# Half masks and two of five rank counts moved from VectorE to ScalarE in a top-k attention and mixture-of-depths kernel

## The chip, the cores and the metric

The kernel runs on one core of a Trainium2 chip. The metric is device microseconds of one execution. Engine names in the profile: PE is TensorE (PEld its weight loads), DVE is VectorE, ACT is ScalarE, POOL is GpSimd, SP is SyncE, which here only issues DMAs. Each engine works through its own queue in order.

## What is computed

There are B = 8 batches, 8 heads, S = 576 tokens and a head size of 64. Attention keeps the 32 largest scores of each row; the result, with the heads side by side, is the input `x` (576 x 512 per batch) of a mixture of depths: a gate picks 128 tokens of each batch, these go through a two-layer network, and the result is added to their rows.

```python
scores = scale * np.matmul(q, k.transpose(0, 1, 3, 2))
kth = np.partition(scores, -32, axis=-1)[..., -32:-31]
attn = softmax(np.where(scores >= kth, scores, -1e9))
x = np.matmul(attn, v)                      # (B, S, H*D)
gate = np.einsum('bsd,d->bs', x, w_gate)
for b in range(B):
    top_idx = np.argpartition(-gate[b], 128)[:128]
    xe = x[b, top_idx]
    ye = np.maximum(xe @ w1, 0.0) @ w2
    out[b, top_idx] = xe + sigmoid(gate[b, top_idx])[:, None] * ye
```

## The kernel before

**Units and steps.** The queries of a batch are cut into five tiles `t`: four of 128 tokens and a last one of 64 (`J` = 4 is the last). One unit is two heads of a tile (or four heads of the short tile), so a batch has 18 units (`per_batch`) and the whole kernel 144. The main loop (line 1143) makes one step per unit and works on units in different stages in each step `n`:

- PE multiplies the scores of unit n+1, and ACT copies them from PSUM to SBUF (`keep`, tile `sc`).
- DVE finds a bound for unit n by MAX8 over sevenths of each row and two rounds over the candidates (`find_bound`, line 527; tiles `cand`, `best`, `bound`).
- ACT takes, for unit n-1, the sign of every score against the bound and sums the signs (`part`, line 561; tiles `sides`, `seen`). POOL multiplies scores by these signs and appends eight steps (`weigh_signs`, tile `y`).
- DVE takes the eight largest of each row of `y` for unit n-2 (`find_kth`, tile `next`); the eighth is the 32nd largest score.
- For unit n-3 the mask of the scores below it is made (`mask`, line 585; tile `less`): the first head by ACT (Relu), the second by POOL. PE adds a large negative number at these places while it transposes the scores in step n+1.
- For unit n-4 ACT takes Exp (`pT`, `last`), PE multiplies by the values, ACT copies the sums out (`xs`).

**The mixture.** When all tiles of a batch have been divided by their sums and their gates computed, `mixture` (line 761) begins. It is a generator that is advanced at written-out steps of the following batches (`mix_at`, line 1023; `mix_at_of` for the last ones). First the gates go to DRAM and come back as a row on all partitions (`gate_row`). Then, for each tile, `choose` (line 800) counts on DVE how many gates of the row are larger than each gate of the tile: its rank. The scratch output is `junk`. A token with rank r goes into slot r, if r < 128: `pick[:, t, :]` is 1 where `slot` equals the rank, made by DVE for tile 0 (line 815) and by POOL for the others (`choose_slot`). PE multiplies `pick` by `parts` (the token's number and its gate, split into three bf16 pieces each), which gives for every slot the token and its gate; ACT copies that to `found`. Then POOL fetches the 128 rows by an indirect DMA, PE runs the two layers in small pieces, and POOL adds the rows to the output by another indirect DMA.

**What sets the order.** The order on each engine is the program's order, written out by hand. Lists hold work back: `vector_late` runs in the middle of the bound's search on DVE, `late` on ACT after the mask of step n (before the copies of loads and `sc`), `pool_late` on POOL after its half mask and before the products `y`. In the six `scatter_steps` (line 1041), in which POOL issues the indirect DMA that adds the rows, the second half mask goes to DVE through `vector_late` instead of POOL (lines 597 to 612 and 1207).

**The end.** The last batch has a path of its own (from line 1278), with counts split into `ranks` and `others`. At the very end DVE reduces a set of checks into `sure` (lines 1489 to 1511): among them, that all ranks and others add up to 8 x 576 x 575 / 2, which holds when no two gates are equal. If a check fails, a branch (line 1641) recomputes all batches in a general way.

Of the kernel before, what the change touches and what calls it, by code (L numbers as in the profile page):

```python
# [10 lines left out]
AF = mybir.ActivationFunctionType  # L11
ALU = mybir.AluOpType
FP32 = mybir.dt.float32
BF16 = mybir.dt.bfloat16
# [5 lines left out]
CAP = 128  # L20
# [28 lines left out]
def kernel(  # L49
# [11 lines left out]
    nc = tc.nc  # L61
    P = nc.NUM_PARTITIONS
    B, H, S, D = q.shape
# [3 lines left out]
    NT = J + 1  # L67
# [3 lines left out]
    DE = D + 1  # L71
    NDC = HD // P
    NFC = F // P
    scale = 1.0 / float(D) ** 0.5 / SMALLER
# [3 lines left out]
    const = ctx.enter_context(tc.tile_pool(name="const", bufs=1))  # L78
# [40 lines left out]
    for i in range(2):  # L119
        gate = const.tile([P, NT], FP32, name=f"gate{i}")  # L120
        nc.gpsimd.memset(gate, 0.0)
        parts = const.tile([P, NT, 2, 3], BF16, name=f"parts{i}")
        nc.gpsimd.memset(parts, 0.0)
        nc.vector.tensor_copy(out=parts[:, :, 0, 0:2], in_=parts_i)
        gates_of.append((gate, parts))
    slot_i = const.tile([P, CAP], I32, name="slot_i")
    nc.gpsimd.iota(slot_i, pattern=[[1, CAP]], base=0, channel_multiplier=0)
# [25 lines left out]

    ranks = const.tile([P, B, NT], FP32, name="ranks")
    nc.gpsimd.memset(ranks, 0.0)

    others = const.tile([P, NT], FP32, name="others")
    nc.gpsimd.memset(others, 0.0)
# [31 lines left out]
    def compare(out, in0, scalar, op, total=None):  # L190
        if total is None:
            total = stats.tile([P, 1], FP32, name="some")[0 : out.shape[0], :]
        dve.tensor_scalar(
            out=out,
            in0=in0,
            scalar1=scalar,
            scalar2=None,
            op0=op,
            op1=ALU.add,
            accum_out=total,  # L200
        )

    late, vector_late, pool_late = [], [], []
# [180 lines left out]
    def bank(pool, name, **how):  # L384
        return pool.tile([P, 512], FP32, name=name, **how)
# [199 lines left out]
    def mask(sc, next8, on=None):  # L585

        less = wkpool.tile([P, 2, S], BF16, name="less")  # L590
        for i, engine in enumerate(on or (act, pool)):
            kth = next8[:, i, 7:8]
            if engine is act:
                act.activation(less[:, i, :], sc[:, i, :], AF.Relu, bias=kth, scale=-1.0)
            else:

                def is_less(engine=engine, i=i, kth=kth):
                    if engine is None:
                        compare(less[:, i, :], sc[:, i, :], kth, ALU.is_lt)
                        return  # L600
                    engine.tensor_scalar(
                        out=less[:, i, :],
                        in0=sc[:, i, :],
                        scalar1=kth,
                        scalar2=None,
                        op0=ALU.is_lt,
                    )

                if engine:
                    is_less()  # L610
                else:
                    vector_late.insert(0, is_less)
        return less

    def turn_some(tr, z, less):
# [142 lines left out]
            rank[0:n, t : t + 1], rank[0:n, t : t + 1], tok[0:n, 1:2], ALU.add  # L758
        )

    def mixture(row0, pg, rank, exact=False):

# [28 lines left out]


        pick = modpool.tile([P, NT, CAP], BF16, name="pick")
        for t in range(NT):
            yield
            n = R if t == J else P

            def choose(t=t, n=n):  # L800
                junk = modpool.tile([P, S], FP32, name="junk", tag="scratch")
                dve.tensor_scalar(
                    out=junk[0:n, :],
                    in0=gate_row[0:n, :],
                    scalar1=gate[0:n, t : t + 1],
                    scalar2=None,
                    op0=ALU.is_gt,
                    op1=ALU.add,
                    accum_out=rank[0:n, t : t + 1],
                )  # L810
                if exact:
                    break_ties(t, gate, gate_row, rank)

                if t == 0:
                    compare(pick[:, t, :], slot, rank[:, t : t + 1], ALU.is_equal)
                else:
                    pool_late.append(lambda: choose_slot(t, n))

            def choose_slot(t, n):
                pool.tensor_scalar(  # L820
                    out=pick[0:n, t, :],
                    in0=slot[0:n, :],
                    scalar1=rank[0:n, t : t + 1],
                    scalar2=None,
                    op0=ALU.is_equal,
                )

            vector_late.append(choose)

# [2 lines left out]
            ps = ps_misc.tile([P, 512], FP32, name="place_ps", tag="misc")  # L832
        else:
            ps = values_bank[0]
        ps = ps[:, 2 * DE : 2 * DE + 6]


        done = B if exact else int(row0) // S + 1
        row_i = modpool.tile([P, 1], I32, name="row_i", bufs=2)
        g = modpool.tile([P, 1], FP32, name="g", bufs=2)  # L840
        multiply_places(ps, pick, pg)
        found = stats.tile([P, 6], FP32, name="found", bufs=2)
        place = stats.tile([P, 2], FP32, name="place", bufs=2)
        kept.append(lambda ps=ps: act.copy(out=found, in_=ps))

# [62 lines left out]
    def multiply_places(ps, pick, pg):  # L908

        for t in range(NT):  # L910
            n = R if t == J else P
            pe.matmul(
                ps,
                pick[0:n, t, :],
                pg[1][0:n, t, :, :].rearrange("p a e -> p (a e)"),
                start=(t == 0),
                stop=(t == J),
            )

    def split(gate, parts):  # L920

        rest = modpool.tile([P, NT], FP32, name="rest")
        pool.tensor_copy(out=parts[:, :, 1, 0], in_=gate)
        pool.tensor_tensor(rest, gate, parts[:, :, 1, 0], ALU.subtract)
        pool.tensor_copy(out=parts[:, :, 1, 1], in_=rest)
        pool.tensor_tensor(rest, rest, parts[:, :, 1, 1], ALU.subtract)
        pool.tensor_copy(out=parts[:, :, 1, 2], in_=rest)

    def add_parts(place, found):
        dve.tensor_reduce(  # L930
            out=place,
            in_=found.rearrange("p (a e) -> p a e", e=3),
            axis=mybir.AxisListType.X,
            op=ALU.add,
        )
# [12 lines left out]
    def fetch_rows(xe, of, row_i):  # L948
        pool.indirect_dma_start(
            out=xe,  # L950
            out_offset=None,
            in_=of.flatten_outer_dims(),
            in_offset=bass.IndirectOffsetOnAxis(ap=row_i, axis=0),
        )
# [182 lines left out]
    def mask_of(n, on=None):  # L1137
        b, i = divmod(n, per_batch)
        masks[n] = mask(scs[n], next8s[b][:, i, :, :], on)
        if i == per_batch - 1 and b < B - 1:  # L1140
            keep_least(b, bounds.pop(b)[:, :, :, 7], next8s.pop(b)[:, :, :, 7])

    for n in range(-1, N):
# [60 lines left out]
        if is_unit(n - 4):  # L1204
            turn_rest()()
        if is_unit(n - 3):
            mask_of(n - 3, (act, None) if n in scatter_steps else None)
        flush()
        if is_unit(n + 1) and n + 1 >= NHP:
            b, i = divmod(n, per_batch)  # L1210
# [55 lines left out]
        if gating is not None:  # L1266
            b, t = gating
            if t == J:
                store(out[b], of_batch[b][0])
                mixtures[b] = mixture(float(b * S), of_batch[b][1], ranks[:, b, :])  # L1270
        for b in rest:
            next(mixtures[b], None)
        b, i = divmod(n, per_batch)
# [153 lines left out]
    for t in (J - 1, J):  # L1427
# [6 lines left out]
            op0=ALU.subtract,  # L1434
            op1=ALU.is_equal,
        )
    ps = bank(ps_end, "av3")[:, 0:6]
    place = stats.tile([P, 2], FP32, name="place", bufs=2)
    row_i = modpool.tile([P, 1], I32, name="row_i", bufs=2)
    g = modpool.tile([P, 1], FP32, name="g", bufs=2)  # L1440
# [2 lines left out]
    keep_rows(place, row_i, float((B - 1) * S), float(B * S - 1))  # L1443
    xe = modpool.tile([P, HD], FP32, name="xe")
    fetch_rows(xe, out, row_i)
    dve.tensor_scalar_max(out=g, in0=place[:, 1:2], scalar1=-88.0)
    act.activation(g, g, AF.Exp, scale=-1.0)
    for _ in between:
# [42 lines left out]
    for what, op, than, limit in (  # L1491
        (bounded, ALU.min, ALU.is_gt, LEAST),
        (least, ALU.min, ALU.is_gt, LEAST),
        (low, ALU.min, ALU.is_gt, 0.5),
        (seen, ALU.max, ALU.is_lt, float(MIDDLE)),
        (seen, ALU.min, ALU.is_gt, float(MIDDLE - 16)),
        (sums.rearrange("p t h -> p (t h)"), ALU.min, ALU.is_gt, FEWEST),
        (sums.rearrange("p t h -> p (t h)"), ALU.max, ALU.is_lt, MOST),
    ):
        far = stats.tile([P, 1], FP32, name="far", bufs=2)  # L1500
        dve.tensor_reduce(out=far, in_=what, axis=mybir.AxisListType.X, op=op)
        dve.scalar_tensor_tensor(
            out=sure, in0=far, scalar=limit, in1=sure, op0=than, op1=ALU.mult
        )

    far = stats.tile([P, 1], FP32, name="far", bufs=2)
    dve.tensor_reduce(out=far, in_=ranks, axis=mybir.AxisListType.XY, op=ALU.add)
    dve.tensor_tensor(sure, sure, far, ALU.add)
    far = stats.tile([P, 1], FP32, name="far", bufs=2)
    dve.tensor_reduce(out=far, in_=others, axis=mybir.AxisListType.X, op=ALU.add)  # L1510
    dve.tensor_tensor(sure, sure, far, ALU.add)
    ones = stats.tile([P, 1], FP32, name="ones", bufs=1)
    dve.memset(ones, 1.0)
    unsure = const.tile([1, 1], I32, name="unsure")
# [2 lines left out]
    for f0 in range(0, NFC, 2):  # L1517
# [20 lines left out]
        out=unsure,  # L1538
        in0=ps[0:1, 0:1],
        scalar1=-1.0,  # L1540
        scalar2=float(P + B * (S * (S - 1) // 2)),
        op0=ALU.mult,
        op1=ALU.add,
    )
# [133 lines left out]
```

## Time and profile before

| | |
|---|---|
| median of 3 runs | 803.54 us (802.9 to 805.48) |
| the profiled execution | 802.83 us; span of its instructions 800.5 us; granted PE clock 0.997 |
| count on DVE (128 or 64 x 576) | 35 in the main loop, 788 ns; 83 ns more to read the accumulator |
| pick on DVE (128 x 128) | 7, 346 ns, and 83 ns |
| half mask on DVE (128 x 576) | 12 (6 in scatter steps, 6 at the end), 797 ns, and 82 ns |
| half mask on ACT | 141, 784 ns |
| half mask on POOL | 135, 1722 ns |
| sign with sum on ACT (`sides`) | 288, 797 ns, and 215 ns to read the accumulator |
| pick on POOL | 21 of 128 partitions, 609 ns |
| ACT_TABLE_LOAD | 1 |

A row of a group or of the timeline names line, engine, operation, what is written `<-` what is read. Most lines are L45, the helper that keeps program order, so groups are told apart by their tiles. In a timeline the first two numbers are the start and the time taken, both in microseconds; a bracket gives idle time of the engine before it and what ended that. Instructions of an engine overlap by a part of their durations, so the distance of two starts is what an instruction costs its queue. A row of waits reads: who, for whom, total in us, how many times, the longest.

### The profile page before, as it was taken

Reading aid. Unit: us, or ns where it says so; the run is one execution under the profiler, and the core shown is the slowest. Engines: PE = TensorE matmul, PEld = TensorE weight load, DVE = VectorE, ACT = ScalarE, POOL = GpSimd, SP = SyncE. Lnnn points to the kernel's source line nnn. Section 1 sums busy time; section 2 is a strip of 40 time slices with the busy share of each in tenths; the row PEclk is TensorE's granted clock in tenths of the full one; section 3 lists DMA queues with packets and bytes.
Section 4 is the critical chain, followed back from the end, with each engine's and each line's share of the span. In section 5 each row is a group of like instructions: output and inputs, shape, how many; then the busy total and the mean of one; then the engine's idle time right before and its main releaser. Section 6 shows DMA issues by size and latency. Waiting matters only on the chain. (4 is left out here: it accounts for less than half of the span.)

```text
span 800.5 us, 33285 instructions
## 1 busy us (share of the span) xinstructions
PE 728.1 (91%) x12535; PEld 550.2 (69%) x12535; DVE 771.6 (96%) x4655; ACT 728.4 (91%) x1577; POOL 706.4 (88%) x722
## 2 busy tenths in 40 slices
PE   8888888788999999999999989999899999999887
PEld 6766666656876668766786667866687667767756
DVE  7999999999999999999999999999999999999962
ACT  6999999999999999999999999999999999989830
POOL 4899999899999999999999999999999999999921
PEclk9999999999999999999999999999999999999999
DMA  8941114121241132221251221502234102101021
GB/s 170 293 95 43 42 62 103 29 54 29 70 107 42 29 94 63 64 55 41 69 109 29 56 41 62 113 20 54 42 90 89 29 8 75 24 6 25 3 74 31
DMA packets 121752, 50.70 MB, mean 63 GB/s; under 512 B 116016, under 2 KB 116016, under 8 KB 120560
## 3 DMA queue, kind: packets, MB, share of 16 engines
q1 hardware_dynamic: 118368, 43.94, 22.2%
q0 software_dynamic: 1744, 4.20, 2.8%
q8 instruction: 101, 1.65, 0.9%
q10 hardware_dynamic: 1472, 0.36, 0.2%
q14 instruction: 67, 0.55, 0.2%
HBM read 36.93 MB, written 11.55 MB: 61 GB/s over the span
## 5 line engine op out<-in xcount | busy, mean ns | idle before, releaser
L45 POOL TENSOR_TENSOR y<-sc,sides 128x576 f32<-128x576 f32 x288 | 366.9, 1304 | 17.7 <-ACT sides L45 16.6
L45 DVE MAX8 cand<-sc 128x8 f32<-128x82 f32 (+1 forms) x2016 | 314.4, 228 | 3.0 <-ACT sc L45 3.0
L45 POOL TENSOR_SCALAR less<-sc,next 128x576 bf16<-128x576 f32 x135 | 232.5, 1722 | 38.4 <-DVE next L45 34.2
L45 ACT ACTIVATE sides<-sc,bound 128x576 bf16<-128x576 f32 x288 | 229.6, 797 | 17.0 <-DVE bound L45 13.1
L45 PEld LDWEIGHTS av<-v,pT 128*64 128x64 f32 x4608 | 146.9, 138 | 91.4 <-ACT last L45 83.8
L45 DVE MAX8 next<-y 128x8 f32<-128x584 f32 x288 | 204.4, 751 | 0.0
L45 PE MATMUL av<-v,pT 128*64 128x65 f32 x4608 | 166.9, 225 | 38.9 <-ACT last L45 38.4
L45 PEld LDWEIGHTS <-less 64*128 64x128 bf16 (+1 forms) x2448 | 157.6, 129 | 29.3 <-POOL less L45 24.6
L45 PE MATMUL ps<-kT,qT 64*128 64x288 f32 (+1 forms) x1248 | 170.1, 422 | 0.3 <-ACT sc L45 0.3
L45 PE MATMUL ptr<-out_of_reach,less 64*128 64x64 bf16 x2272 | 151.0, 190 | 17.3 <-POOL less L45 16.6
L45 PE MATMUL ptr<-ident,sc 64*128 64x64 f32 x2272 | 166.3, 252 | 0.0
L45 ACT ACTIVATE pT<-ptr 128x1024 f32<-128x1024 f32 x142 | 147.7, 1040 | 14.5 <-PE ptr L45 12.7
L45 ACT COPY sc<-ps 128x1152 f32<-128x1152 f32 x140 | 159.6, 1140 | 0.0
L45 PEld LDWEIGHTS ptr<-ident,sc 64*128 64x128 f32 x2272 | 138.6, 137 | 23.8 <-issue 21.2
L45 ACT ACTIVATE less<-sc,next 128x576 bf16<-128x576 f32 x141 | 110.5, 784 | 0.0
L45 PEld LDWEIGHTS ps<-kT,qT 64*128 64x128 f32 (+1 forms) x1248 | 92.8, 176 | 17.6 <-ACT sc L45 0.4
L45 DVE MATCH_REPLACE8 cand<-best,cand 128x21 f32<-128x21 f32 (+1 forms) x576 | 98.8, 179 | 0.0
L45 DVE MAX8 best<-cand 128x8 f32<-128x21 f32 (+1 forms) x576 | 90.4, 189 | 0.0
L45 ACT ACTIVATION_READ_ACCUMULATOR sides<-sc,bound 128x1 f32 x288 | 62.0, 215 | 0.0
L45 PE MATMUL h_ps<-xeT,w 128*128 128x128 f32 x464 | 61.9, 278 | 0.0
L45 PEld LDWEIGHTS av<-ident,sc 128*128 128x128 f32 x144 | 20.0, 139 | 54.8 <-issue 44.9
L45 PE MATMUL av<-vpair,last 128*64 128x130 f32 x576 | 56.9, 276 | 0.0
(165 smaller groups left out, 925.2 us busy)
## 6 DMA issues: line engine op xcount, KB each, us to landing
v<-in_v_dram SPq DMA_DIRECT2D x64, 128.0 KB, 3.7
out_dram<-x SPq DMA_DIRECT2D x8, 1024.0 KB, 4.1
rows<-in_k_dram SPq DMA_DIRECT2D x56, 128.0 KB, 2.8
rows<-in_q_dram SPq DMA_DIRECT2D x56, 128.0 KB, 2.9
w<-in_moe_w_dram SPq DMA_DIRECT2D x2, 2048.0 KB, 10.3
gate_row<-row_dram SPq DMA_DIRECT2D x7, 288.0 KB, 4.6
last<-in_q_dram SPq DMA_DIRECT2D x8, 128.0 KB, 3.6
vpair<-in_v_dram SPq DMA_DIRECT2D x16, 64.0 KB, 4.8
```

The costliest lines, as they stand in the source:

```text
L45: return lambda *a, **kw: self._tc.keep_in_program_order(fn(*a, **kw))
```

## The change

**Half mask.** In the scatter steps both half masks are made by ACT (Relu, as the first half always was); DVE makes none in the main loop.

**Ranks of tiles 0 and 1.** In batches 0 to 6 DVE no longer counts for these two tiles. ACT takes the sign of (gate minus each gate of the row), with its sum: the sum is the number of smaller gates less the number of larger ones, 575 - 2 x rank. It is queued through `late`; its scratch output is the front of `pick`, which is filled later. The sums land in `signs`.

**Slots.** POOL compares `slot_signs` (575 - 2 x slot) with these sums, for both tiles after the sign of tile 1. So POOL makes the pick of tile 0, too. Tiles 2 to 4 stay as they were.

**Check.** `parts` has a seventh column of ones, so the matmul also tells how many tokens each slot got; ACT's copy goes to `places`, one row of seven numbers for each batch. At the end two reductions ask that each of these counts lies between 0.5 and 1.5; they stand in place of the two sums of ranks.

In the queues this means: per batch, DVE loses two counts and a pick (and in six steps a mask), ACT gets two signs (and in six steps a mask), POOL gets one pick. The order of everything else in the main loop stays.

```diff
@@ mask
-                def is_less(engine=engine, i=i, kth=kth):
-                    if engine is None:
-                        compare(less[:, i, :], sc[:, i, :], kth, ALU.is_lt)
-                        return
...
-                if engine:
-                    is_less()
-                else:
-                    vector_late.insert(0, is_less)
+                engine.tensor_scalar(
+                    out=less[:, i, :],
+                    in0=sc[:, i, :],
+                    scalar1=kth,
+                    scalar2=None,
+                    op0=ALU.is_lt,
+                )
@@ mixture
+            def weigh_gates(t=t):
+                total = sign_sum[:, t : t + 1]
+                act.activation(
+                    pick.rearrange("p t c -> p (t c)")[:, 0:S],
+                    gate_row,
+                    AF.Sign,
+                    bias=gate[:, t : t + 1],
+                    scale=-1.0,
+                    accum_out=total,
+                )
+                if t == 1:
+                    for u in range(2):
+                        pool_late.append(
+                            lambda u=u: choose_slot(
+                                u, P, slot_signs, sign_sum[:, u : u + 1]
+                            )
+                        )
+
+            if t < 2 and not exact:
+                late.append(weigh_gates)
+                continue
...
-                if t == 0:
-                    compare(pick[:, t, :], slot, rank[:, t : t + 1], ALU.is_equal)
-                else:
-                    pool_late.append(lambda: choose_slot(t, n))
+                pool_late.append(lambda: choose_slot(t, n))
...
-        found = stats.tile([P, 6], FP32, name="found", bufs=2)
+        found = places[:, 0 if exact else done - 1, :]
@@ main loop
-            mask_of(n - 3, (act, None) if n in scatter_steps else None)
+            mask_of(n - 3, (act, act) if n in scatter_steps else None)
@@ last batch
+    act.copy(out=places[:, B - 1, 6:7], in_=ps[:, 6:7])
@@ checks at the end
+        (places[:, :, 6], ALU.min, ALU.is_gt, 0.5),
+        (places[:, :, 6], ALU.max, ALU.is_lt, 1.5),
...
-    dve.tensor_reduce(out=far, in_=ranks, axis=mybir.AxisListType.XY, op=ALU.add)
-    dve.tensor_tensor(sure, sure, far, ALU.add)
...
-    dve.tensor_reduce(out=far, in_=others, axis=mybir.AxisListType.X, op=ALU.add)
-    dve.tensor_tensor(sure, sure, far, ALU.add)
```

At the start four instructions are new: DVE makes `slot_signs` from `slot`, POOL sets the ones of both `parts` tiles and the whole of `places`.

## Prediction

> **What bounds the kernel now.** First the page's busy times, to see which engine could be the bound.
>
> ```profile
> PE 728.1 (91%) x12535; PEld 550.2 (69%) x12535; DVE 771.6 (96%) x4655; ACT 728.4 (91%) x1577; POOL 706.4 (88%) x722
> ```
>
> Four engines lie within 8% of one another, so an average decides nothing. The loop works batch by batch (18 steps), so next I cut out one settled batch (steps 72 to 89, from the DVE timeline) and asked for busy time by stretch, then for ACT's waits in it.
>
> ```profile
> 377.17:471.75 94.58, 89.32 (x1555) 66.89 (x1553) 94.44 (x576) 90.92 (x198) 88.18 (x88) 1.00 0.26 61
> ```
>
> The columns are window, length, then busy PE, PEld, DVE, ACT, POOL. DVE is idle 0.14 us of 94.58: its instruction count sets the period. ACT has 3.66 us free. Its waits:
>
> ```profile
> ACT sides L45 <- DVE bound L45: 2.2, 5, 0.6
> ACT pT L45 <- PE ptr L45: 0.8, 2, 0.5
> ```
>
> ACT waits mostly for DVE; the same question for DVE in this batch lists no wait at all. Third, the DVE timeline of step 8 and the start of step 9, with the work the change touches:
>
> ```profile
> 417.83 1.10 DVE L45 MAX8 cand<-sc 128x8 f32<-128x82 f32 x7
> 418.95 0.76 DVE L45 TENSOR_SCALAR_CACHE_REDUCE junk<-gate_row,gate 128x576 f32<-128x576 f32 x1
> 419.75 0.35 DVE L45 TENSOR_SCALAR_CACHE_REDUCE pick<-slot,ranks 128x128 bf16<-128x128 f32 x1
> 420.02 1.11 DVE L45 MAX8 cand<-sc 128x8 f32<-128x82 f32 x7
> 423.76 1.39 DVE L45 MAX8 cand<-sc 128x8 f32<-128x82 f32 x9
> ```
>
> The rank count and the pick stand between two halves of the candidate search, with nothing beside them on DVE. Fourth, what such a step costs against one without (step 6, 8, 10, 12):
>
> ```profile
> 408.35:413.09 4.74, 4.74 (x89) 3.92 (x88) 4.74 (x32) 4.74 (x12) 4.16 (x8) 1.00 0.90 193
> 417.83:423.76 5.93, 5.93 (x100) 5.08 (x98) 5.89 (x37) 5.89 (x14) 5.93 (x6) 1.00 0.21 46
> 429.11:434.58 5.47, 5.07 (x88) 3.42 (x86) 5.47 (x34) 4.93 (x11) 4.98 (x5) 1.00 0.00 0
> 440.05:444.86 4.81, 4.60 (x82) 3.21 (x78) 4.81 (x33) 4.76 (x11) 4.53 (x4) 1.00 0.01 3
> ```
>
> Step 6 is bare, step 12 has only a reciprocal, step 8 reciprocal, count and pick, step 10 one count. So a count is worth 5.47 − 4.74 = 0.73 us, and count plus pick 5.93 − 4.81 = 1.12 us. Last, ACT's queue at the start of such a batch:
>
> ```profile
> 379.66 1.04 ACT L45 ACTIVATE pT<-ptr 128x1024 f32<-128x1024 f32 x1
> 381.36 0.78 ACT L45 ACTIVATE sides<-sc,bound 128x576 bf16<-128x576 f32 x1 [0.65 <-DVE bound L45]
> 382.04 0.19 ACT L45 ACTIVATION_READ_ACCUMULATOR sides<-sc,bound 128x1 f32 x1
> 382.13 0.26 ACT L45 ACTIVATE last<-av 128x128 f32<-128x128 f32 x1
> 382.29 0.76 ACT L45 ACTIVATE less<-sc,next 128x576 bf16<-128x576 f32 x1
> 382.95 0.63 ACT L45 COPY kT<-ps 128x256 f32<-128x256 f32 x2
> ```
>
> Instructions overlap, so starts count, not durations: a sign with its accumulator takes 382.13 − 381.36 = 0.77 us, a mask 382.95 − 382.29 = 0.66.
>
> **Part 1: what DVE loses.** Seven batches (0 to 6) each lose a count plus pick (1.12) and a second count (0.73): 7 × 1.85 = 12.95 us. The six scatter steps lose the half mask; such a step (377.17 to 382.64) is 5.47 long against 4.74, so 6 × 0.73 = 4.38. Sum 17.3 us, all on the engine that sets the period. By the page's durations it would be more (788 + 83 and 346 + 83 and 797 + 82 ns: 20.7 us), but those overlap their neighbours; I keep 17.3 and use the larger sum for the low end only.
>
> **Part 2: what ACT gains.** Two signs with accumulator and, where a scatter falls, one mask: 2 × 0.77 + 0.66 = 2.2 us per batch, 14.7 us over the run. ACT works in order; behind the added sign stand the kT/qT copies, the sc copy (the next DVE step and the next score matmuls of PE wait for it), the second sign (POOL's y) and the xs copy. Each is 0.77 later in steps 8 and 10. DVE doesn't feel that as long as the leads hold: the sc copy of step 8 began at 419.36 and took 1.14, so ended at 420.50, and DVE used it at 423.76, 3.26 us later. POOL's y ended at least 2.25 us before DVE's next in every step of this batch.
>
> Over a batch, DVE's period becomes 94.58 − 1.85 − 0.73 = 92.0. Does ACT fit in that? By busy time 90.92 + 2.2 = 93.1: it doesn't. But busy time overstates it: an instruction that follows a wait loses its overlap. Above, pT starts at 379.66 and the waiting sign at 381.36, 1.70 us; where nothing waits pT holds the queue for 0.92. The slack there is 0.78, though 0.65 is shown. There are 22 idle stretches of ACT in the batch; with 0.12 more for each the slack is 3.66 + 2.6 = 6.3 us. The change asks for 2.2 + 2.58 = 4.8. It fits, with some 1.5 us left, at most half of which I would trust (ACT also pauses after the xs copies). Within the batch ACT is already up to 0.95 us late in steps 1 to 4 and 7; adding 0.77 while DVE's step gets shorter (1.12 in step 8, 0.73 in step 10) brings the peak to about 2.3 us around step 10, then steps 11 to 17 take it back. 2.3 is under the 3.26 of sc. It is near the lead of y, but in steps 8 to 11 that is 3.3 to 4.8.
>
> A rule speaks against this: the Trainium skill, "ScalarE: Activation LUTs", section "Rules for kernel authors", wants simple elementwise work on VectorE, up to about three times faster there. If each ACT instruction cost three times DVE's 0.73, ACT would gain 6.6 us a batch, need up to 97.5, and the kernel would end some 20 us slower. The rows say otherwise: at fp32 and 576 wide a sign takes 0.77 on ACT and a count 0.73 on DVE. I take the rows.
>
> **Part 3: POOL, PE and DMA.** POOL takes over the first pick (609 ns, 0.57 between starts), and tile 1's, which it already did, now waits for ACT's second sign in step 10. Queued behind it is the y pair; POOL got to this pick at 431.08, and the sign should end about 430.3 plus ACT's lateness. That delays y by 2 us at worst, inside its lead of 3.3 or more. POOL has 6.4 us free per batch, 3.2 after the change. PE's place matmuls get a seventh column (165 ns rows): nothing measurable. PE no longer waits for DVE's late half mask (3.0 us in six waits); that slack goes back to ACT. The gate row is needed no earlier in ACT's queue than about 2 us after its landing (last one issued 690.41, at most 5.3 to land, ACT there at 697.86).
>
> **Part 4: both ends.** The start gains one DVE instruction (about 0.23 us by the row of out_of_reach) in front of a 1.05 us wait for PE, and three small POOL memsets before a wait of 9.9 us: nothing, or 0.3 if that cover failed. At the end two reduces and two adds give way to two reduces and two compares (0.15 to 0.19 each): nothing. The new ACT copy (about 0.18) stands before the gate's Exp, where ACT idled 0.85. ACT may enter the tail a little later; for that and stray stalls I allow 0.3 us.
>
> **Sum.** 17.3 − 0.3 = 17.0. The profiled execution took 802.83 (span 800.5), giving 785.8. The median of the runs is 803.54, 0.71 above it: 786.5.
>
> **Rivals.** Full gain (0.70): as above, 784.5 to 789.5.
> ACT becomes the bound (0.25): if busy time is ACT's true need, the period is 93.1, the gain 1.5 × 7 = 10.3, the time 793.2. For it: ACT shows 90.9 busy of 94.6, and part of its stalls on PE may be unavoidable. Against: step 6 ran both engines in 4.74 without idling.
> The fallback runs (0.03), and the kernel is slower. The end now demands that each of the 128 slots of a batch was matched once. A rank is now a sum of signs with one exact zero, a gate against itself; if Sign gave 1 there, the sum would be odd where the slot's number isn't, tiles 0 and 1 would match nothing, and the branch behind the check would redo everything. Its DVE price: per half unit four MAX8 and three replaces of 576 elements at about 0.67 each, plus 0.7, so 5.4 us; 288 of them are 1.55 ms, ending near 2350 us. One lost slot decides. The trace can't exclude it: its only Sign is scaled to avoid zero. The skill's page named above ("Step-by-step: what each stage is for") says that zeros go to a constant of each function after a singly rounded affine, which makes zero likely; no run here shows it.
> No change that can be measured (0.02): several stalls eat nearly all.
>
> **Chances and range.** A measurement of this kernel can tell about 0.3% (2.4 us) from no change. Faster 0.95, same 0.02, slower 0.03. The range 784.5 to 793.5 takes in both forecasts on the fast side and leaves out the fallback and larger stalls.
>
> **What would show it.** Right: DVE still without waits in a middle batch, its period near 92.0; steps 8, 10 and 0 near 4.8; ACT busy near 743 and its waits for DVE's bound nearly gone; the sc copy still over 1 us ahead of DVE. Wrong: DVE waits for sc or for y, periods near 93, or POOL waiting at pick with y late behind it.

## The result, and the profile after

The changed kernel takes 791.27 us (median of 4 runs, 791.16 to 792.41) against 804.27 us for the kernel before, run beside it (802.9 to 805.48): a ratio of 0.984 [0.982, 0.986], 13.0 us faster. 17.0 were forecast. The time is inside the range and on the forecast side; the gain is a quarter short, and the document is about that quarter. The profiled execution took 791.16 us (span 788.8), 11.7 less than before by the same measure.

The busy times of the changed kernel:

```profile
PE 722.0 (92%) x12535; PEld 548.0 (69%) x12535; DVE 761.3 (97%) x4602; ACT 735.6 (93%) x1612; POOL 721.4 (91%) x732
```

DVE has 53 instructions fewer, but lost only 10.3 us of busy time. POOL, which was to gain 7 picks of 0.57 us, some 4 us, and otherwise to keep its work, gained 15. The batch of steps 72 to 89 by stretch (window, length, busy PE, PEld, DVE, ACT, POOL), the same batch as was shown of before:

```profile
372.62:465.69 93.07, 88.58 (x1549) 66.69 (x1549) 92.97 (x569) 91.87 (x203) 90.78 (x89) 1.00 0.27 62
```

The period fell from 94.58 to 93.07; 92.0 were forecast. DVE is idle 0.10 us of it, and lists no wait in this batch, as before. So DVE still sets the period, yet takes 1.07 us longer than its work was reckoned at. The single steps say where. These are steps 6, 8, 9, 10, 12 and 13 of that batch, and below them steps 9 and 13 of the kernel before:

```profile
403.56:408.29 4.73, 4.73 (x89) 3.92 (x88) 4.73 (x32) 4.73 (x11) 4.43 (x10) 1.00 0.74 169
412.38:417.19 4.81, 4.54 (x88) 3.63 (x84) 4.81 (x33) 4.81 (x11) 4.81 (x6) 1.00 0.45 101
417.19:423.09 5.90, 5.80 (x96) 4.65 (x96) 5.90 (x33) 5.90 (x15) 5.77 (x6) 1.00 0.21 47
423.09:427.83 4.74, 4.37 (x80) 3.01 (x78) 4.74 (x31) 4.74 (x10) 4.46 (x6) 1.00 0.00 0
433.31:438.11 4.80, 4.74 (x84) 3.25 (x82) 4.80 (x33) 4.80 (x12) 4.80 (x6) 1.00 0.02 4
438.11:444.29 6.18, 5.58 (x89) 3.61 (x85) 6.18 (x34) 5.66 (x12) 6.18 (x6) 1.00 0.38 86
```

```profile
423.76:429.11 5.35, 5.26 (x90) 3.62 (x90) 5.35 (x34) 5.09 (x12) 4.60 (x6) 1.00 0.23 54
444.86:450.35 5.49, 5.12 (x85) 3.64 (x84) 5.49 (x34) 4.94 (x11) 5.22 (x6) 1.00 0.43 97
```

Steps 8 and 10 came out as reckoned (4.81 and 4.74, from 5.93 and 5.47). Steps 9 and 13, in which the change removes nothing, went from 5.35 and 5.49 to 5.90 and 6.18. DVE is busy throughout, so no view of waits shows this. The timelines do. Step 13 on DVE, and then POOL beside it:

```profile
438.11 1.39 DVE L45 MAX8 cand<-sc 128x8 f32<-128x82 f32 x9
439.41 1.50 DVE L45 CUSTOM_DVE_ANT_0 prod<-x,wg 128x512 f32<-128x512 f32 x1
440.85 0.82 DVE L45 MAX8 cand<-sc 128x8 f32<-128x82 f32 x5
```

```profile
437.81 2.52 POOL L45 TENSOR_TENSOR y<-sc,sides 128x576 f32<-128x576 f32 x2
440.29 0.70 POOL L45 TENSOR_TENSOR y<-steps,seen 128x16 f32<-128x16 f32 x1
440.98 1.72 POOL L45 TENSOR_SCALAR less<-sc,next 128x576 bf16<-128x576 f32 x1
```

The same place in the kernel before, DVE and POOL:

```profile
446.17 0.81 DVE L45 CUSTOM_DVE_ANT_0 prod<-x,wg 128x512 f32<-128x512 f32 x1
```

```profile
443.02 2.52 POOL L45 TENSOR_TENSOR y<-sc,sides 128x576 f32<-128x576 f32 x2
445.50 0.22 POOL L45 TENSOR_TENSOR y<-steps,seen 128x16 f32<-128x16 f32 x1
445.69 1.73 POOL L45 TENSOR_SCALAR less<-sc,next 128x576 bf16<-128x576 f32 x1
```

`prod` is the dot product of a tile's rows `x` with the gate's weights, one DVE instruction that reads two tensors in SBUF. Before, POOL's pair `y` had ended at 445.54 when it started. After, POOL is in the middle of the pair, and the dot product takes 1.50 instead of 0.81: it ends at 440.91, 0.58 after `y` has ended at 440.33. POOL's next instruction, the small `y<-steps,seen`, then takes 0.70 instead of 0.22 and ends at 440.99, just behind the dot product. Each holds the other, and the waiting is hidden in a longer duration. POOL's half masks lose in the same way where one starts just behind a dot product (2.2 us instead of 1.72). That is why both engines look busier. Over the run, the group of the 32 full tiles, after and then before (count, then busy us, mean ns, idle before):

```profile
L45 DVE CUSTOM_DVE_ANT_0 prod<-x,wg 128x512 f32<-128x512 f32 x32 | 31.3, 978 | 0.1
```

```profile
L45 DVE CUSTOM_DVE_ANT_0 prod<-x,wg 128x512 f32<-128x512 f32 x32 | 24.1, 753 | 0.1
```

With the 8 short tiles (5.9 us against 6.4) all dot products took 37.2 us after and 30.5 before: 6.7 more. 1.7 of it is a single one, in step 9 of the last batch (2.37 instead of 0.67). From the first search of step 0 to that of step 143 the trace has 743.55 us before and 732.75 after, 10.8 less; 17.3 − 6.7 = 10.6. The end from step 143 gained 1.1 (49.3 to 48.2: DVE waited 2.5 us for `sums` there, and now 0.9), and the start lost 0.25.

### The profile page after: what moved, and what is told of

Its sections match the earlier page's. It is cut to its first block, busy times and chain, and to the rows that moved or that the text cites. A ratio compares the mean times of both kernels' runs of the same rounds, so it can differ in the third digit from the quotient of the medians.

```text
span 788.8 us, 33265 instructions
## 1 busy us (share of the span) xinstructions
PE 722.0 (92%) x12535; PEld 548.0 (69%) x12535; DVE 761.3 (97%) x4602; ACT 735.6 (93%) x1612; POOL 721.4 (91%) x732
## 5 line engine op out<-in xcount | busy, mean ns | idle before, releaser
L45 POOL TENSOR_SCALAR less<-sc,next 128x576 bf16<-128x576 f32 x135 | 237.9, 1762 | 6.1 <-DVE next L45 4.4
L45 ACT ACTIVATE sides<-sc,bound 128x576 bf16<-128x576 f32 x288 | 232.5, 808 | 0.8 <-DVE bound L45 0.7
L45 PEld LDWEIGHTS av<-v,pT 128*64 128x64 f32 x4608 | 146.1, 137 | 92.6 <-ACT last L45 81.9
L45 PEld LDWEIGHTS <-less 64*128 64x128 bf16 (+1 forms) x2448 | 160.5, 131 | 12.2 <-POOL less L45 9.8
L45 ACT COPY sc<-ps 128x1152 f32<-128x1152 f32 x140 | 161.8, 1156 | 0.0
L45 PE MATMUL ptr<-ident,sc 64*128 64x64 f32 x2272 | 159.6, 252 | 0.0
L45 PE MATMUL ptr<-out_of_reach,less 64*128 64x64 bf16 x2272 | 146.7, 189 | 7.7 <-POOL less L45 7.5
L45 ACT ACTIVATE less<-sc,next 128x576 bf16<-128x576 f32 x147 | 116.4, 796 | 0.0
L45 ACT ACTIVATION_READ_ACCUMULATOR sides<-sc,bound 128x1 f32 x288 | 65.7, 228 | 0.0
L45 PE MATMUL y_ps<-w,hT 128*128 128x512 f32 x112 | 56.6, 600 | 0.0
```

Of the source, the lines that this page charges most:

```text
L45: return lambda *a, **kw: self._tc.keep_in_program_order(fn(*a, **kw))
```

## The experiments

**Theory 1.** DVE's dot product can't run while POOL runs its two-input product `y`. ACT's new work makes POOL later against DVE, so that `y` now lies under the dot products of steps 9 and 13 (tiles 0 and 1), and this costs the 6.7 us. **Theory 2**, the rival, is the second forecast on record: ACT's added work as such is what costs, through the copies and signs that come later, and the long dot products are only where a loss shows that would come anyway. Theory 2 says that the place of the dot product doesn't matter, and that only ACT's load does.

The kernel before took 803.12 us beside the first four and 803.25 beside the others.

**Move the dot product, in both kernels.** The dot products of tiles 0 and 1 are moved from the middle of the search to just behind it, some 2.1 us later on DVE (in the step shown, the rest of the search lasts from 440.85 to 442.95). No other instruction changes. In the changed kernel (`dot_late`) and in the kernel before (`before_dot_late`):

```diff
+    gates_late = []
-            amid_late.append(lambda a=gating: gates(*a))
+            (gates_late if gating[1] < 2 else amid_late).append(
+                lambda a=gating: gates(*a)
+            )
...
             bound_of(n)
+        while gates_late:
+            gates_late.pop(0)()
```

> The changed kernel, with the gate's dot product of the first two tiles moved on DVE from the middle of the candidate search to just after the bound; nothing else changes on any engine. Theory 1 (the missing 4 us are DVE's dot product waiting while POOL's product y runs): in steps 9 and 13 POOL is then in its half mask, the dot products fall back from 1.23 and 1.50 us to about 0.7, the period of a middle batch from 93.07 to about 92.0, the time from 791.3 to 784.5 to 786.5. Theory 2 (ACT is the bound, at 91.9 us busy of 93.07): the place of the dot product on DVE does not matter, 790.5 to 791.5.

> The kernel before, with the same move. There POOL runs y, not the half mask, at the new place. Theory 1: the dot products of steps 9 and 13 grow from 0.67 and 0.82 us to about 1.5, some 1.5 us a batch, 7 to 12 us in all: 811 to 816. Theory 2 (two-input work of DVE and POOL does not disturb each other): 803 to 805.

`dot_late` took 803.83 us, ratio 1.001 [1.000, 1.002]: this move alone gives the whole gain back. `before_dot_late` took 809.74, ratio 1.009 [1.007, 1.010]. Theory 2 as stated is out: ACT's work is the same and the place decides 12.6 us. Theory 1's numbers were wrong too, by far for `dot_late` and by little for `before_dot_late` (811 to 816). For `dot_late` it had placed POOL as it stood in the trace after, but POOL's place against DVE changes with every collision. Step 13 of a middle batch of `dot_late`, DVE and POOL:

```profile
447.34 2.65 DVE L45 CUSTOM_DVE_ANT_0 prod<-x,wg 128x512 f32<-128x512 f32 x1
```

```profile
446.91 2.54 POOL L45 TENSOR_TENSOR y<-sc,sides 128x576 f32<-128x576 f32 x2
449.38 0.68 POOL L45 TENSOR_TENSOR y<-steps,seen 128x16 f32<-128x16 f32 x1
```

The row of POOL is two products in sequence; here DVE doesn't get in between them and waits for both (449.45, plus 0.54). In step 13 of `before_dot_late` it does get in: the dot product takes 0.96, and the second product 1.73 instead of 1.27. What decides that isn't shown. Step 9 of `before_dot_late` shows the wait with the second product already running:

```profile
429.87 1.62 DVE L45 CUSTOM_DVE_ANT_0 prod<-x,wg 128x512 f32<-128x512 f32 x1
```

```profile
428.42 2.52 POOL L45 TENSOR_TENSOR y<-sc,sides 128x576 f32<-128x576 f32 x2
430.90 0.67 POOL L45 TENSOR_TENSOR y<-steps,seen 128x16 f32<-128x16 f32 x1
```

It ends 0.55 after `y`. The sums agree with the times: all dot products together take 49.5 us in `dot_late`, 12.3 more than after, and the time is 12.6 more; 37.3 in `before_dot_late`, 6.8 more than before, and the time is 6.6 more.

**Each part of the change alone.** `mask_only` is the kernel before with the half mask of the scatter steps on ACT; `signs_only` is the changed kernel with that half mask still on DVE.

```diff
-            mask_of(n - 3, (act, None) if n in scatter_steps else None)
+            mask_of(n - 3, (act, act) if n in scatter_steps else None)
```

> The kernel before, with only the half mask of the six scatter steps moved from DVE to ACT. The sum predicted 4.4 us less: 799.9. Theory 1: no more than one small new collision, since POOL has slack here: 799.5 to 801. Theory 2: ACT has 3.66 us free and needs 0.66 of it: the same 799.9.

> The changed kernel, with the half mask of the scatter steps left on DVE as before; only the rank signs, the slots and the check are changed. The sum predicted 12.95 us less than before: 791.3. Theory 1: most of the collisions of steps 9 and 13 stay, since POOL has the same extra pick and the same short steps 8 and 10: loses 4 to 6 of it, 795 to 797. Theory 2: ACT needs 92.5 a batch where DVE needs 92.7, so DVE stays the bound: 791 to 792.5.

`mask_only`: 800.13 us, 0.996 [0.995, 0.998], 3.0 less. In a middle batch (step 90 on) step 0 lost 0.73 as reckoned and step 8 gained 0.08; the batch takes 93.95 instead of 94.57. `signs_only`: 792.59, 0.987 [0.985, 0.988], 10.5 less; a middle batch takes 92.74, which is 94.58 − 1.85 and 0.01, and its dot products in steps 9 and 13 are as short as before (0.67 and 0.83). Theory 1 had expected its collisions to remain here, and they don't, except for 1.27 in one early batch and 1.88 in step 9 of the last one; the time is 0.1 above Theory 2's 791 to 792.5. So in a middle batch it takes both parts together: the mask adds 0.66 us to ACT in step 0, nine steps ahead of the place where POOL then comes too late. The sizes fit, too: of the 12.95 us reckoned for the signs 2.4 are missing, and the dot products took 1.8 more than before; of the 4.4 for the mask 1.4 are missing, of which 0.8 are dot products and some 0.35 the 0.08 or so in step 8 of four batches. By the whole times the two parts add up to 13.5 us, hardly more than the 13.0 of both together. In the loop from step 0 to 143 they add up to 14.4 (3.2 and 11.25) against 10.8; the stretch from step 143 on hides most of that, since it took 49.7 and 50.2 in these two profiles and 48.2 after.

**Other places for the same work.** If Theory 1 holds, placing the dot products where POOL isn't at `y` wins time with all of ACT's load kept. `dots_in_phase` puts tile 0's dot product off from step 9 to 15 and tile 1's from 13 to 16, where the trace after has POOL at its half mask:

```diff
+    dots_at = {}
...
-            amid_late.append(lambda a=gating: gates(*a))
+            wait = {0: 6, 1: 3}.get(gating[1], 0)
+            dots_at.setdefault(n + wait, []).append(lambda a=gating: gates(*a))
+        amid_late.extend(dots_at.pop(n, ()))
```

> The changed kernel, with the gate dot products of tiles 0 and 1 put off from steps 9 and 13 to steps 15 and 16, at the same place within DVE's step; there POOL is in its half mask, well past its start, in every run so far. Theory 1 (collision with POOL's y is the whole loss): both cost 0.67 us, the middle batch falls from 93.07 to 92.0, the dot products from 37.2 to 28 us in all, the time to 782 to 785. Theory 2 (ACT is the bound once the collisions are gone, because sc comes only 0.1 us ahead in step 9): DVE waits for sc in steps 9 to 11 instead, the middle batch stays over 92.6, the time at 787 to 790.

787.61 us (786.67 to 788.06), ratio 0.981 [0.979, 0.982]: faster than both kernels; the interval lies below that of the changed kernel's own second series (0.982 to 0.985, below). The time is Theory 2's (787 to 790) and not Theory 1's (782 to 785), while the batch fits neither ("over 92.6", 92.0). The batch of steps 90 to 107:

```profile
463.79:556.22 92.43, 88.47 (x1551) 66.66 (x1551) 92.33 (x568) 91.84 (x203) 88.91 (x89) 1.00 0.26 63
```

ACT's 91.84 is the same as after, POOL is 1.7 us less busy than in this batch after (90.64), and the period is 0.63 shorter (93.06). The waits for `sc` that Theory 2 named hardly appear: DVE is idle 0.10 us. All dot products take 31.6 us, 5.6 less than after; the loop from step 0 to 143 is 4.4 shorter. The one in step 15 still takes 1.01, since it starts 0.27 behind POOL's half mask:

```profile
540.76 1.01 DVE L45 CUSTOM_DVE_ANT_0 prod<-x,wg 128x512 f32<-128x512 f32 x1
```

```profile
540.49 1.73 POOL L45 TENSOR_SCALAR less<-sc,next 128x576 bf16<-128x576 f32 x1
```

It ended at 541.77, while the half mask ran on to 542.22. A half mask holds the dot product for its first 0.6 us or so (0.27 + 1.01, less the 0.67 that the dot product takes alone), not for its whole length. `dots_16_17` puts tile 0's dot product into step 17 and leaves tile 1's in 16 (in the last batch 15 and 16). Against `dots_in_phase`, and with DVE's search taking all dot products of a step instead of one:

```diff
-                if (i, u) == (1, 2) and amid_late:
-                    amid_late.pop()()
+                if (i, u) == (1, 2):
+                    while amid_late:
+                        amid_late.pop(0)()
...
-            wait = {0: 6, 1: 3}.get(gating[1], 0)
+            wait = {0: 8 if gating[0] < B - 1 else 6, 1: 3}.get(gating[1], 0)
```

> The changed kernel, with the gate dot product of tile 0 put off to step 17 (next to tile 2's) and that of tile 1 to step 16 (in the last batch steps 15 and 16). In the run with steps 15 and 16 the one in step 15 still took 1.01 us, since POOL's half mask had only just begun. Theory 1: every dot product of a middle batch at 0.67 to 0.83 us, the period 92.0 to 92.15, the time 784.5 to 786.5. Theory 2 (ACT is the bound once the dot products are out of the way; sc was 0.03 us ahead of DVE in step 11): DVE waits for sc or y in steps 11 to 15, the period stays at 92.4 or more, 787 to 789.

789.76 us, 0.983 [0.981, 0.984]; a middle batch takes 92.61, the dot products 31.9 together. Theory 1 had 784.5 to 786.5, Theory 2 787 to 789. It is no better than `dots_in_phase`: step 16 now meets the start of the half mask (1.13), and step 17 carries two dot products with 0.14 us of idle time.

**Other places on ACT.** `signs_23` gives ACT the ranks of tiles 2 and 3 (steps 11 and 14) instead of 0 and 1, so that it is less late in steps 8 to 10. The scratch output of these signs is a buffer of its own, and the two picks follow (not shown):

```diff
-            if t < 2 and not exact:
+            if t in (2, 3) and not exact:
```

> The changed kernel, with ACT's signs made for tiles 2 and 3 (steps 11 and 14) instead of tiles 0 and 1 (steps 8 and 10), and DVE counting tiles 0, 1 and 4; the amount of work on each engine is the same. Theory 1: ACT and POOL, late from the scatter step's mask, get steps 8 and 10 to catch up, the dot products of steps 9 and 13 stay near 0.7 to 1.0 us, the middle batch at 92.0 to 92.4, the time 784 to 787. Theory 2 (ACT's total work of 91.9 a batch is the bound, wherever it stands): no change, 790.5 to 792.

792.25 us, 0.987 [0.985, 0.989], as Theory 2 had it (790.5 to 792); Theory 1 had 784 to 787. A middle batch takes 92.7. The collisions stay, at 1.15 in step 9 and 1.13 in step 13, and the dot products take 36.8 together. Step 8 has no added sign here, so what makes POOL late in step 9 is there before it; Theory 1 had expected that one step without the sign would clear it. `signs_last` leaves tiles 0 and 1, but runs the added sign behind the second `sides` of the step instead of ahead of the `sc` copy:

```diff
-                late.append(weigh_gates)
+                signs_late.append(weigh_gates)
...
             sign(n - 1, 1)
+        while signs_late:
+            signs_late.pop(0)()
```

> The changed kernel, with ACT's rank signs put behind the second sign of the step instead of ahead of the copies, so that the copies to sc and POOL's second sign are not held up in that step. Theory 1: POOL is in its own queue in step 8 anyway, and its pick in step 10 waits about 2 us longer with y behind it, so the collision of step 13 grows: 791 to 794. Theory 2 (what stands behind the sign in ACT's queue, sc above all, is what costs): 786 to 789.

807.11 us, 1.005 [1.004, 1.007]: slower than the kernel before, and far from both numbers (791 to 794, 786 to 789). Here POOL's picks wait for the added sign:

```profile
POOL pick L45 <- ACT pick L45: 15.7, 7, 2.3
```

(who, for whom: us in all, times, the longest). Behind them `y` is late, and it meets the dot product of step 13, which takes up to 3.04 there and 4.14 in step 9 of the last batch; 48.4 us in all, 11.2 more than after. DVE's waits for `sc`, `y` and `sums` grew by 3.4. Together that is 14.6 of the 16.0 us between the two spans.

**The changed kernel again.**

> The changed kernel itself, beside the run above on the same chip: 791 to 792 by both theories.

790.36 us (790.07 to 791.77), 0.984 [0.982, 0.985]. In this profile the same program collides at other places: 0.67 in step 9, 1.22 in step 13, 0.96 in step 3 (behind the start of a half mask), and a middle batch takes 92.68. The dot products take 35.3 in all, and the end from step 143 50.8. The pattern is stable over the middle batches of one execution, but not between executions.

**What the theories are worth.** The time came out inside Theory 2's numbers or within 1 us of them in five of the eight variants, and of Theory 1's in one. What speaks for the collisions is not Theory 1's forecasts but the traces: moving the dot product alone, both ways, changes the time, and the durations of the dot products account for the change. What is left of Theory 2 is that ACT's work decides where POOL stands.

## Why the forecast was right, and where it was short

The time lies in the range because the range was drawn up to 793.5 to take in "ACT becomes the bound", which isn't what happened; that much is luck. The forecast of the full gain itself, 784.5 to 789.5, was missed. By the prediction's own signs its reading was wrong in part: it named periods near 93 as such a sign, and 93.07 was measured.

**Part 1 was right.** The count, pick and half mask are worth what the step windows gave: 1.84 of 1.85 us a batch in `signs_only`, 0.73 in step 0 of `mask_only`. (The sum by the page's durations is 20.5 and not 20.7; only the low end was drawn from it.)

**Part 2 failed in one sentence:** "DVE doesn't feel that as long as the leads hold." The leads did hold, barely (`sc` still came 0.14 us ahead of its use in step 9, so "still over 1 us ahead" was wrong), and ACT's lateness was about as forecast: it peaked at 2.8 us in step 8 and was 2.6 in step 10, against 2.3. (It stood at 2.0 to 2.3 as early as steps 1 to 4, up to 0.95 before: the walk through the batch left out the mask of step 0.) But a lead is about data only. DVE felt the lateness by another way: a late ACT makes a late POOL, and a late POOL has `y` running when DVE wants its dot product. Over the run, POOL's waits for DVE, before and then after, show that POOL went from being ahead of DVE to being behind it:

```profile
POOL less L45 <- DVE next L45: 34.2, 62, 1.0
```

```profile
POOL less L45 <- DVE next L45: 4.4, 12, 0.7
```

In the middle batch POOL waits for ACT's `sides` once, 1.0 us in step 1, and from there to step 13 it is idle for only 0.7 us, so it can't catch up. Part 3 counted 3.2 us of POOL's time as free after the change (2.3 were), but took that only as room for a later `y`. How much of the lateness is ACT's and how much is POOL's own full queue, no run separates.

The reading needs DVE and POOL laid side by side around every instruction of DVE with two inputs in SBUF, which the prediction didn't do. It looked at `y` only for when it ends before `next` needs it. The sentence of Part 3, that the delay of `y` stays "inside its lead", has the same fault.

**The missing term.** For the middle batch: 92.0, plus 1.23 − 0.67 in step 9, plus 1.50 − 0.82 in step 13, minus 0.13 for step 5, where a brush with the half mask went away, gives 93.1; measured are 93.07. For the run the term is 6.7 us, and the end gave 1.1 more than the 0 that Part 4 had: 785.8 + 6.7 − 1.1 = 791.4 against 791.16 profiled. In the second profile of the same kernel the term is 4.8 and the end lost 1.5: 785.8 + 4.8 + 1.5 = 792.1 against 791.77. For the loop from step 0 to 143 alone, 743.55 less the work taken off DVE plus what the dot products took more gives 731.0 in `after_again`, 745.2 in `dot_late`, 732.4 in `signs_only` and 750.4 in `before_dot_late`; the traces have 731.1, 745.2, 732.3 and 750.5. The sum falls short by 0.4 to 1.0 in `mask_only`, `signs_23` and `dots_in_phase`, and by 2.6 and 3.5 in `dots_16_17` and `signs_last`, where DVE also waits.

**"ACT becomes the bound" named a close time, 793.2, for the wrong reason.** ACT's idle time in a middle batch is 1.2 us, and its busy time grew by only 0.95 there (90.92 to 91.87) for the 2.2 us of work added, so busy time did overstate its need, as Part 2 had argued. `dots_in_phase` does all of ACT's work in a period 0.63 shorter. ACT's waits for DVE's bound in the whole run, before and then after:

```profile
ACT sides L45 <- DVE bound L45: 13.1, 28, 1.3
```

```profile
ACT sides L45 <- DVE bound L45: 0.7, 1, 0.7
```

ACT has become the engine that comes second, and through its order the one that places POOL, but DVE's own instructions fill the period.

**The fallback didn't run:** DVE has 4602 instructions, so the redo isn't among them, and the sign of a gate against itself was 0. The choice of the rows over the skill's figure of three was right: the added signs take 794 ns each on ACT, the counts on DVE 795. But the skill never spoke against this change. The Trainium skill, "ScalarE: Activation LUTs", section "Rules for kernel authors", gives that figure for bf16 with a single source in 4× mode, a condition that the prediction left out, and these rows are fp32.

**Open:** why `dots_in_phase` stays at 92.43 where 92.0 were reckoned. Its steps 15 and 16 cost 0.20 more than its steps 9 and 13 saved, step 3 costs 0.13 and step 10 0.08; which of this a better place would take back wasn't found by the one further try. The room may be small: in the middle batches of both kernels `sc` comes 0.03 us ahead of its use in step 11, so ACT is about to become the bound there.

## What to carry to other kernels

When work moves from the bounding engine to another, list the instructions of DVE with two inputs in SBUF and the instructions of POOL beside them, in each step, before and after the expected shift: a delay that every lead absorbs can still push the two onto each other. The view of waits stays empty then; look for one group whose mean duration has grown while its shape is the same. Such an instruction is worth moving to a step in which POOL does something else, even six steps later, if its result isn't due.

## What the runs showed of the hardware

- **DVE and POOL exclude each other for these instructions.** In each case shown, the dot product ended 0.54 to 0.58 us after the end of POOL's `y`, wherever it had started, and POOL's next `y<-steps,seen` took 0.67 to 0.70 instead of 0.22. The Trainium skill, "SBUF — State Buffer", section "Who interferes with whom", says that a DVE instruction with two SBUF inputs contends with a GpSimd instruction that reads SBUF, because its second input comes through a read interface that the two share; the section "SBUF: two separate sides" of the same page adds that whichever starts first holds the shared pair for its whole instruction and the other is blocked. The trace agrees for `y`.
- **An instruction of DVE with one SBUF tensor as input isn't held.** A rank count ran beside the second product of `y` in step 11 of the changed kernel in its usual time, as the page's section "Who interferes with whom" has it:

```profile
428.85 0.80 DVE L45 TENSOR_SCALAR_CACHE_REDUCE junk<-gate_row,gate 128x576 f32<-128x576 f32 x1
```

```profile
427.49 2.53 POOL L45 TENSOR_TENSOR y<-sc,sides 128x576 f32<-128x576 f32 x2
```

- **For the half mask the page's "whole instruction" doesn't hold.** POOL's half mask lasts 1.72 us. In the profiles kept, a dot product of a full tile that started 0.04 to 0.6 us behind the mask's start ended some 1.3 us after that start (one 1.42), and one that started later took its 0.67 or 0.68, but for one of 0.80 and one that was caught by the next `y`.
- **The loser can lose twice.** Two products of POOL in sequence held the dot product 2 us (2.65 taken, 0.67 alone); in another case it got in between them.
- **A collision shifts the next one.** A held dot product makes DVE later against POOL, so the number for `dot_late` couldn't be had from the trace of another kernel; and two executions of one program fell into different patterns. What sets the pattern of an execution is not shown.
